# The three pieces of w_out converted inside the mixing steps, in the memory of theta's weights

## The chip, the cores and the metric

The kernel runs on one core of a Trainium2 chip. The metric is the device time of one execution in microseconds (us), the median of several runs; lower is better. The names of the engines are those of the profile: PE (matmul), PEld (its weight loads), DVE (vector), ACT (scalar), POOL (GpSimd) and SP, whose queue issues all the transfers.

## The reference, cut to what matters

Three layers follow each other. The first is an mLSTM-like attention with gates over 4 batches, 8 heads, 768 tokens and a head size of 40. Its output, 4 x 768 x 320, goes through a mixing layer, and that one's output through a gated convolution:

```python
theta = x @ w_theta                      # 320 x 320
zr, zi = x * cos(theta), x * sin(theta)
y = einsum('ts,bsd->btd', w_tok_r, zr) + einsum('ts,bsd->btd', w_tok_i, zi)   # 768 x 768 each
u = x + y
x = u + maximum(u @ w_ch, 0)             # 320 x 320
gate_pre = sum(conv_w[k] * x shifted by 4 - k tokens for k in range(5))
out = (sigmoid(gate_pre) * (x @ w_val)) @ w_out                               # 320 x 320 each
```

All weights arrive as 64-bit floating point numbers and are turned into 32-bit ones on the core. w_out is used by the last product alone.

## The kernel before, in words

The attention works through 12 groups (`attend(d)`; each is one batch's third of the tokens). Per group there are matrix products of gates (`weigh`), of keys and queries (`scores`), of states (`carry`, `inter`, `numer`), and a tail on DVE and POOL (`finish`). `weigh` ends in two exponentials on ACT, one for each half p of the heads (`W_m<-bank` or `x_b<-bank` in the profile).

The mixing layer has 24 steps (`step(n)`, recorded by two loops at the end): 2 pairs of batches (p), 2 halves of the output tokens, 6 chunks of the input tokens. A step issues 30 matmuls (`mix`, `bank<-wt_m,z` in the profile), and has the weights of the next step made (`weight`): for the first pair of batches a transfer of 64-bit numbers (`r_b<-in_wtok_dram`), ACT and DVE instructions that make 32-bit ones (`r_b<-r_b`) and split them into a high and a low part (`wt_m<-r_b`), and a transfer that keeps the parts in DRAM for the second pair (`wt_dr<-wt_m`). `theta(p, c)` makes the angles and with them z, the other operand of mix; for the first pair it reads w_theta from `w_t`. After six steps of a half its product with w_ch follows (`f_ch`), with DVE's convolution, then the one with w_val (`f_val`) and at last the one with w_out (`f_out`), each of them in the middle of the next half's mix steps.

The other weights are converted in 13 pieces by `cv_piece`: three of w_theta, the convolution's (cw), and three each of w_ch, w_val and w_out. A piece is a transfer of 320 KB (128 x 320 numbers of 8 bytes), one copy with scaling on ACT (`xq_m<-xq_m`), on DVE one TENSOR_SCALAR (shift) and two SCALAR_TENSOR_TENSOR (insert the low bits, insert the sign), and for w_ch, w_val and w_out another copy on ACT (`out_hi`) and a subtraction on DVE or POOL (`out_lo`). All pieces share two buffers in `xq_m`, used in turn.

The order of all this is not that of the code. Every call is recorded in a plan, and `Plan.order` lists the recorded steps: it takes costs, dependencies and due times (the time at which PE wants the result, worked back) and picks again and again the engine that is free first and its most urgent step. For some operations it also picks the engine (`any2`: DVE or POOL; `copy`: ACT or DVE). One table of the program acts on the pieces: `BY` says for a group of the attention which piece has to be done before the group's first exponential (`plan.follow`). Before, pieces 0 to 12 are all tied to groups 3 to 10, the last one to group 10. Each engine then carries out its own list in order.

Of the kernel before, what the change touches and what calls it, by code (L numbers as in the profile page):

```python
# [11 lines left out]
I64 = mybir.dt.int64  # L12
# [6 lines left out]
DM = H * D  # L19
# [10 lines left out]
WARM = 7  # L30
RFIRST = (1,)
GATES = (0, 2, 4)
BY = {3: 0, 4: 1, 5: 3, 6: 4, 7: 6, 8: 8, 9: 10, 10: 12}
U = L // 2
NU2 = S // U
FAR = -32768.0
# [311 lines left out]
def tile_kernel(ctx, tc, qT, kT, kt, v1, og, ig, fg, w_th, w_ch, w_val, w_out, cw, wtok,  # L348
# [12 lines left out]
    def turn(kind, n):  # L361

        turns[kind] = turns.get(kind, -1) + 1
        return turns[kind] % n

    def words(n, name, dtype=F32, place=None, bufs=1):

        t = sb.tile([128, n], dtype, name=name, tag=place or name, bufs=bufs)
        k = turn(place, bufs) if place else 0
        plan.place[t.name] = f"{place or name}.{k}"  # L370
        return t
# [12 lines left out]
    w_t = [words(n * DM, f"w_t{bb}").rearrange("p (k n) -> p k n", k=n) for bb, n in ((0, 3), (1, 1))]  # L384
# [34 lines left out]
    def cv_scale(raw, m):  # L419
        hi = raw.bitcast(I32).rearrange("p (n t) -> p n t", t=2)[:, :, 1]  # L420
        act.activation(out=m, in_=hi.bitcast(F32), func=AF.Copy, scale=REBIAS)

    def cv_bits(raw, m):
        w = raw.bitcast(I32).rearrange("p (n t) -> p n t", t=2)
        mi = m.bitcast(I32)
        dve.tensor_scalar(out=mi, in0=mi, scalar1=3, scalar2=None, op0=ALU.logical_shift_left)
        dve.scalar_tensor_tensor(out=mi, in0=w[:, :, 0], scalar=29, in1=mi,
                                 op0=ALU.logical_shift_right, op1=ALU.bitwise_or)
        dve.scalar_tensor_tensor(out=mi, in0=w[:, :, 1], scalar=-2147483648, in1=mi,
                                 op0=ALU.bitwise_and, op1=ALU.bitwise_or)  # L430
# [55 lines left out]
    def weigh(g):  # L486
# [8 lines left out]
        for p in range(2):  # L495
# [14 lines left out]
            act.activation(out=W[:, p], in_=G_ps, func=AF.Exp)  # L510
            if p == 0 and g in BY:
                plan.follow(made[BY[g]])
        st["W", g] = W
# [112 lines left out]
    def cv_piece(nm, src, k_):  # L626
        t = turn("cv", 2)
        raw = xq_m[:, (8 + 2 * t) * DM:(10 + 2 * t) * DM].bitcast(I64)
        v = xq_m[:, (12 + t) * DM:(13 + t) * DM]
        if nm == "cw":  # L630
            raw, v = raw[:, 0:15], cw_sb.rearrange("p j t -> p (j t)")
        sp.dma_start(out=raw, in_=src if nm == "cw" else src[:, k_ * DM:(k_ + 1) * DM])
        cv_scale(raw, v)
        cv_bits(raw, v)
        made.append(cw_sb[:] if nm == "cw" else w_t[0][0:64, k_] if nm == "th" else wsp[nm][1][:, k_])
        if nm == "cw":
            return
        if nm == "th":
            w0 = w_t[0][:, k_]
            if k_ == 2:  # L640
                pool.memset(w0[64:], 0.0)
                pool.memset(w_t[1][0:64], 0.0)
                act.activation(out=w_t[1][64:, 0], in_=v[64:], func=AF.Copy, scale=INV2PI)
                w0, v = w0[0:64], v[0:64]
            dve.tensor_scalar(out=w0, in0=v, scalar1=INV2PI, scalar2=None, op0=ALU.mult)
            return
        hi, lo = wsp[nm]
        act.activation(out=hi[:, k_, 0:DM], in_=v, func=AF.Copy)
        n = DM if nm == "out" else 256
        any2.tensor_tensor(out=lo[:, k_], in0=v[:, 0:n], in1=hi[:, k_, 0:n].bitcast(F32),  # L650
                           op=ALU.subtract)
        if n < DM:
            any2.tensor_tensor(out=hi[:, k_, DM:384], in0=v[:, 256:DM],
                               in1=hi[:, k_, 256:DM].bitcast(F32), op=ALU.subtract)

    pieces = [(nm, src, k_) for nm, src in (("th", w_th), ("ch", w_ch), ("val", w_val),
                                            ("out", w_out)) for k_ in range(3)]
# [256 lines left out]
    def mix(p, th_i, c, js=range(5)):  # L914
        z_hi, z_lo = st["z", p, c]
        w_hi, w_lo = st["w", p, th_i, c]
        for j in js:
            y = bank[j][:, 0:TH]
            with plan.joined():
                for ri in range(2):  # L920
                    zh, zl = blk(z_hi[:, ri], j), blk(z_lo[:, ri], j)
                    first = c == 0 and ri == 0
                    last = c == NC - 1 and ri == 1
                    pe.matmul(y, zh, w_hi[:, ri], start=first, stop=False)
                    pe.matmul(y, zh, w_lo[:, ri], start=False, stop=False)
                    pe.matmul(y, zl, w_hi[:, ri], start=False, stop=last)
# [53 lines left out]
    def f_u(p, th_i, bb):  # L980
        for j in ((0, 1, 4), (2, 3))[bb]:
            for g3 in (th_i, th_i + 1):
                a, e = max(0, 2 * g3 - 3 * th_i), min(3, 2 * g3 + 2 - 3 * th_i)
                i = 3 * th_i + a - 2 * g3
                old, y, new = (xq[p][:, 2 * g3:2 * g3 + 2, j, i * U:(i + e - a) * U].rearrange("p u (i l) -> p i u l", l=U),
                               *(t[:, a * L:e * L].rearrange("p (i u l) -> p i u l", u=2, l=U)
                                 for t in (bank[j], u_f[:, j])))
                dve.tensor_tensor(out=new, in0=old, in1=y, op=ALU.add)
        split(u_f, bb)
# [82 lines left out]
    def step(n):  # L1072

        half, k = divmod(n, NC)
        half -= 1
        fh = divmod(half, 2)
        if half == 2 and k == 0:
            both = words(12 * DM, "hl_x", F32R, place="x1")
            hl_x = both[:, 0:8 * TH].rearrange("p (s j t) -> p s j t", s=2, j=4)
            sr_x = both[:, 8 * TH:].rearrange("p (j t) -> p j t", j=2)  # L1080
            parts.append(part[:])
            part[:] = [[hl_x[:, s, 2 * bb:2 * bb + 2] for bb in range(2)] for s in range(2)] + [sr_x]
        if half >= 0 and k == 0:
            f_u(*fh, 0)
            f_u(*fh, 1)
        if 0 <= n < NS - 2:
            mix(*seq[n])
        elif n >= NS - 2:
            mix(*seq[n], (0, 1, 4))
        if half >= 0:  # L1090
            d = int(half == 0)
            if k == d:
                f_ch(*fh)
            elif k == 3 + d:
                f_val()
            elif k == 5 and half < 1:
                f_out(*fh, part, ob6)
        if 0 <= n + 1 < NS:
            weight(*seq[n + 1])
        if n == 7:  # L1100
            theta_weights()
        if n in first_use:
            theta(*first_use[n])

    parts = []
    todo = iter(pieces)
    for d in range(-1, NG):
        attend(d)
        for piece in [next(todo, None) for _ in range(1 + (d > 1 and d % 2 == 0))]:
# [3 lines left out]
    stage[0] = 1  # L1113
    for n in range(NS):
        step(n)
    stage[0] = 2

    parts.append(part[:])
# [82 lines left out]
```

## Time and profile before

| what | value |
|---|---|
| median of 3 runs | 398.55 us (396.32 to 399.29) |
| profiled execution | 394.67 us, of which its span is 392.8 us |
| PE busy | 355.9 us of the span |
| DVE, ACT, POOL busy | 328.8, 210.5, 95.1 us |
| TensorE clock granted, mean | 0.948 of 2.4 GHz |
| transferred | 57.74 MB |

The span is the time from the first instruction to the last on the profiled core. The profiled execution is 3.88 us under the median of the three timed runs.

The page's strip of 40 slices (9.8 us each) shows two stages: until about 147 us, where the attention goes on, PE is at 4 to 9 tenths; from about 150 us on it is full to the end, since the mix steps keep it so.

### The profile page before, as it was taken

The numbers are of one execution on the slowest core, as the hardware profiler recorded it, in microseconds if no ns is written. First come the engines' busy times: TensorE is split into PE (matmuls) and PEld (weight loads), VectorE is DVE, ScalarE is ACT, GpSimd is POOL, SyncE is SP. The second block draws the span as 40 slices with busy tenths as digits, with TensorE's granted clock in tenths as the row PEclk, the third lists the DMA queues.
The fourth block names the chain that finished last, engine by engine and source line by source line (L and its number), as shares of the span: only waits on it lengthen the run. The fifth ranks groups of instructions, "written<-read, shape, count | busy, mean of one in ns | idle before, by whom it ended". The sixth has DMA issues, their size and how long they took to land.

```text
span 392.8 us, 11329 instructions
## 1 busy us (share of the span) xinstructions
PE 355.9 (91%) x4736; PEld 325.0 (83%) x4736; DVE 328.8 (84%) x675; ACT 210.5 (54%) x373; POOL 95.1 (24%) x112
## 2 busy tenths in 40 slices
PE   4879888577878879999999999999999999999996
PEld 3556756466665658999999999999999999999996
DVE  7987959779989989999889988859987679468990
ACT  3655145025664776866544558865686332335463
POOL 8132322214646430100110033040022110213320
PEclk9585669988999999999999999999999999999999
DMA  5987749887655084969794184221320410000214
GB/s 168 301 230 216 210 139 244 204 227 202 195 164 147 9 237 119 294 192 270 210 300 164 61 257 163 85 81 38 124 82 18 152 73 0 2 0 2 101 38 164
DMA packets 22386, 57.74 MB, mean 147 GB/s; under 512 B 2912, under 2 KB 9216, under 8 KB 22336
## 3 DMA queue, kind: packets, MB, share of 16 engines
q1 hardware_dynamic: 22336, 57.03, 49.4%
q8 instruction: 37, 0.61, 0.7%
q14 instruction: 13, 0.11, 0.1%
HBM read 43.65 MB, written 13.37 MB: 145 GB/s over the span
## 4 chain that ended last, share of the span: by engine, by line
PE 52%; DVE 28%; ACT 8%; issue 7%; DMA 3%; POOL 0%; SPq 0%; ACTq 0%; DVEq 0%
PE bank L66 52%; DVE k_m L66 6%; DVE th_m L66 4%; DVE r_b L66 4%; DVE num_m L66 3%; DMA r_b<-in_wtok_dram 3%; ACT th_m L66 2%; DVE z L66 2%; DVE wt_m L66 1%; DVE xq_m L66 1%; ACT L66 1%; DVE g_m L66 1%; DVE f_m L66 1%; ACT W_m L66 1%; DVE W_m L66 1%
## 5 line engine op out<-in xcount | busy, mean ns | idle before, releaser
L66 PE MATMUL bank<-wt_m,z 128*128 128x384 f32 x480 | 87.6, 338 | 0.1
L66 PEld LDWEIGHTS bank<-wt_m,z 128*128 128x128 f32 x480 | 83.3, 188 | 0.8 <-DVE z L66 0.4
L66 PE MATMUL bank<-w_r,z 128*128 128x384 f32 x240 | 43.3, 336 | 0.0
L66 DVE SCALAR_TENSOR_TENSOR k_m<-k_m,cw_sb,k_m 128x384 f32<-128x384 f32 (+1 forms) x52 | 41.3, 830 | 0.4
L66 PEld LDWEIGHTS bank<-w_r,z 128*128 128x128 f32 x240 | 41.5, 188 | 0.0
L66 POOL TENSOR_TENSOR kw_m<-r_b,ewc 128x320 f32<-128x320 f32 x20 | 17.4, 873 | 40.6 <-PE bank L66 27.3
L66 PE MATMUL bank<-r_b,kw_m 64*64 64x41 f32 (+1 forms) x704 | 20.4, 236 | 7.1 <-DVE f_m L66 4.2
L66 PEld LDWEIGHTS bank<-r_b,kw_m 64*64 64x64 f32 (+1 forms) x704 | 17.4, 145 | 9.0 <-DVE f_m L66 4.3
L66 PE MATMUL bank<-q_m,k_m 64*64 64x64 f32 x768 | 18.8, 246 | 6.2 <-issue 5.8
L66 DVE SCALAR_TENSOR_TENSOR r_b<-r_b,r_b 128x768 int32<-128x768 int32 x24 | 23.7, 992 | 0.2
L66 DVE TENSOR_TENSOR k_m<-k_m,bank 104x164 f32<-104x164 f32 (+1 forms) x36 | 14.9, 420 | 9.4 <-PE bank L66 6.8
L66 PEld LDWEIGHTS bank<-q_m,k_m 64*64 64x64 f32 x768 | 16.5, 156 | 7.3 <-issue 6.2
L66 POOL TENSOR_TENSOR hl_f<-k_m,hl_f 128x768 fp32r<-128x768 f32 x4 | 8.1, 2030 | 55.8 <-ACT hl_f L66 55.8
L66 ACT ACTIVATE th_m<-bank,magic 128x320 f32<-128x320 f32 x24 | 12.5, 522 | 15.9 <-DVE th_m L66 9.0
L66 PE MATMUL bank<-w_t,xq_m 128*128 128x320 f32 x72 | 20.7, 437 | 0.3 <-ACT xq_m L66 0.3
L66 ACT ACTIVATE th_m<-th_m 128x640 f32<-128x640 f32 (+1 forms) x27 | 19.0, 702 | 3.3 <-DVE th_m L66 2.6
L66 ACT ACTIVATE z<-th_m 128x640 fp32r<-128x640 f32 x24 | 16.8, 730 | 6.2 <-DVE th_m L66 6.1
L66 ACT ACTIVATE W_m<-bank 128x512 f32<-128x512 f32 x16 | 9.3, 594 | 18.5 <-PE bank L66 18.5
L66 ACT ACTIVATE ewc<-bank 64x384 f32<-64x384 f32 x16 | 7.8, 486 | 21.1 <-PE bank L66 20.9
L66 ACT ACTIVATE xq_m<-bank 128x512 f32<-128x512 f32 (+2 forms) x36 | 14.7, 431 | 6.6 <-PE bank L66 5.5
L66 ACT ACT_TABLE_LOAD x14 | 18.0, 1283 | 0.3
L66 PEld LDWEIGHTS bank<-w_t,xq_m 128*128 128x128 f32 x72 | 13.4, 190 | 5.3 <-ACT xq_m L66 0.4
(207 smaller groups left out, 911.7 us busy)
## 6 DMA issues: line engine op xcount, KB each, us to landing
r_b<-in_wtok_dram SPq DMA_DIRECT2D x24, 384.0 KB
wt_dr<-wt_m SPq DMA_DIRECT2D x12, 768.0 KB
w_r<-wt_dr SPq DMA_DIRECT2D x8, 768.0 KB
r_b<-in_v_dram SPq DMA_DIRECT2D x12, 328.0 KB
q_m<-in_qT_dram SPq DMA_DIRECT2D x24, 160.0 KB
k_m<-in_kT_dram SPq DMA_DIRECT2D x24, 160.0 KB
r_b<-in_kt_dram SPq DMA_DIRECT2D x12, 320.0 KB
wt_m<-wt_dr SPq DMA_DIRECT2D x4, 768.0 KB
```

The source lines that it names most:

```text
L66: calls[u] = lambda e=e: getattr(e, op)(*args, **kw)
```

## The change

`cv_piece` gets other buffers for the three pieces of w_out: both the 64-bit numbers and the converted piece lie in `w_t[0]`, where theta's weights are for the first pair of batches. The three pieces have this one buffer among them, and none can be loaded before the last matmul that reads theta's weights there. Their recording moves from the attention's loop to mix steps 8, 9 and 10 (`OUT_AT`). The ten other pieces stay with the attention's groups, and `BY` spreads them over groups 3 to 10. The number of pieces and of their instructions stays as it is.

```diff
-BY = {3: 0, 4: 1, 5: 3, 6: 4, 7: 6, 8: 8, 9: 10, 10: 12}
+BY = {3: 0, 4: 1, 5: 2, 6: 4, 7: 5, 8: 7, 9: 8, 10: 9}
+OUT_AT = (8, 9, 10)
...
         t = turn("cv", 2)
         raw = xq_m[:, (8 + 2 * t) * DM:(10 + 2 * t) * DM].bitcast(I64)
         v = xq_m[:, (12 + t) * DM:(13 + t) * DM]
+        if nm == "out":
+            t3 = w_t[0].rearrange("p k n -> p (k n)")
+            raw, v = t3[:, 0:2 * DM].bitcast(I64), t3[:, 2 * DM:]
...
-    todo = iter(pieces)
+    todo = iter(pieces[:-3])
...
     for n in range(NS):
         step(n)
+        if n in OUT_AT:
+            cv_piece(*pieces[n - OUT_AT[0] - 3])
```

Since the plan is made anew, the order changes from the first microseconds on, on every engine; from the first w_ch product on, PE's order is the one of before. DVE's list has 671 instructions where it had 677, POOL's 120 for 117 and ACT's 383 for 375: some operations changed engines, and ACT's list has 20 loads of a function table where it had 15. Up to the end of the attention there are 15 of them for 10.

ACT around the exponentials of attention group 10 (`W_m<-bank_98` and `W_m<-bank_99`, its two halves; the `th_m<-th_m` rows are the sine and the absolute value of theta, `z` its result's high part). Before:

```order
L66 ACTIVATE th_m<-bank_98,magic 128x320
L66 ACTIVATE out_hi<-xq_m 128x320
L66 ACTIVATE z<-th_m 128x640
L66 ACTIVATE th_m<-bank_99,magic 128x320
L66 ACT_TABLE_LOAD
L66 ACTIVATE W_m<-bank_98 128x512
L66 ACTIVATE z<-th_m 128x640
L66 ACTIVATE W_m<-bank_99 128x512
L66 ACTIVATE r_b_81<-r_b_79 128x768
```

With the change:

```order
L67 ACTIVATE th_m<-bank_98,magic 128x320
L67 ACTIVATE th_m<-bank_99,magic 128x320
L67 ACTIVATE W_m<-bank_98 128x512
L67 ACT_TABLE_LOAD
L67 ACTIVATE th_m<-th_m 128x640 x2
L67 ACTIVATE th_m<-th_m,halfpi 128x640
L67 ACT_TABLE_LOAD
L67 ACTIVATE W_m<-bank_99 128x512
L67 ACTIVATE r_b_81<-r_b_79 128x768
```

Between the two halves of one group now stand two table loads and the three activations of a theta; `out_hi` is gone from here.

DVE just ahead of the last weights that it splits for the first pair of batches (`wt_m_107<-r_b_81`, made for mix step 11). Before:

```order
L66 TENSOR_TENSOR sr_f<-k_m_82,sr_f 64x384
L66 TENSOR_SCALAR r_b_81<-r_b_81 128x768
L66 SCALAR_TENSOR_TENSOR r_b_81<-r_b_80,r_b_81 128x768
L66 SCALAR_TENSOR_TENSOR th_m<-th_m,bank_105 128x256
L66 SCALAR_TENSOR_TENSOR th_m<-th_m,bank_105 128x64
L66 SCALAR_TENSOR_TENSOR r_b_81<-r_b_80,r_b_81 128x768
L66 TENSOR_TENSOR k_m_83<-k_m_83,bank_103 128x384
L66 TENSOR_TENSOR wt_m_107<-r_b_81,wt_m_107 128x768
```

With the change:

```order
L67 TENSOR_TENSOR sr_f<-k_m_82,sr_f 64x384
L67 TENSOR_SCALAR r_b_81<-r_b_81 128x768
L67 TENSOR_SCALAR w_t_70<-w_t_70 128x320
L67 SCALAR_TENSOR_TENSOR r_b_81<-r_b_80,r_b_81 128x768
L67 SCALAR_TENSOR_TENSOR w_t_70<-w_t_70 128x320
L67 SCALAR_TENSOR_TENSOR r_b_81<-r_b_80,r_b_81 128x768
L67 SCALAR_TENSOR_TENSOR th_m<-th_m,bank_105 128x256
L67 SCALAR_TENSOR_TENSOR th_m<-th_m,bank_105 128x64
L67 TENSOR_TENSOR k_m_83<-k_m_83,bank_103 128x384
L67 SCALAR_TENSOR_TENSOR w_t_70<-w_t_70 128x320
L67 TENSOR_TENSOR wt_m_107<-r_b_81,wt_m_107 128x768
```

The third piece's three instructions now stand among these; the first and the second stand in the same way earlier in the mix steps.

SP's queue in the mix steps with the change (`w_t_70<-in_w_out_dram` are the three pieces; `wt_m_106` and `wt_m_107` are the two buffers of the split weights). Before, the same transfers stand there without the pieces:

```order
L67 DMA r_b_79<-in_wtok_dram 64x2x384 x2
L67 DMA w_t_70<-in_w_out_dram 128x320
L67 DMA r_b_80<-in_wtok_dram 64x2x384 x2
L67 DMA wt_dr<-wt_m_106 128x1536
L67 DMA w_t_70<-in_w_out_dram 128x320
L67 DMA wt_dr<-wt_m_107 128x1536
L67 DMA r_b_79<-in_wtok_dram 64x2x384 x2
L67 DMA wt_dr<-wt_m_106 128x1536
L67 DMA r_b_80<-in_wtok_dram 64x2x384 x2
```

The second piece, which waits until the first is converted, now stands ahead of a store and of the next raw weights.

## Rows read from the trace of the kernel before

**Rows 1.** The page, part 1: busy time and share by engine.

```profile
PE 355.9 (91%) x4736; PEld 325.0 (83%) x4736; DVE 328.8 (84%) x675; ACT 210.5 (54%) x373; POOL 95.1 (24%) x112
```

**Rows 2.** Windows: stretch, length, busy us per engine, granted clock, DMA share, GB/s.

```profile
core 0: us, PE busy (x) PEld busy (x) DVE busy (x) ACT busy (x) POOL busy (x), PEclk, DMA share, GB/s
85.00:147.00 62.00, 51.21 (x1524) 39.42 (x1523) 58.56 (x137) 38.70 (x65) 29.89 (x35) 0.96 0.60 165
147.00:184.00 37.00, 36.95 (x197) 33.74 (x198) 35.96 (x63) 26.49 (x41) 1.68 (x2) 1.00 0.73 214
184.00:230.00 46.00, 46.00 (x270) 45.69 (x268) 42.56 (x68) 21.04 (x33) 4.45 (x4) 1.00 0.63 192
230.00:282.00 52.00, 50.97 (x320) 50.04 (x318) 43.16 (x82) 36.97 (x70) 11.02 (x10) 1.00 0.32 109
```

**Rows 3.** Groups of DVE's instructions, 85 to 184 us: busy, mean ns, idle before.

```profile
L66 DVE SCALAR_TENSOR_TENSOR xq_m<-xq_m 128x320 int32<-128x320 int32 x16 | 10.0, 626 | 0.1
...
L66 DVE TENSOR_SCALAR xq_m<-xq_m 128x320 int32<-128x320 int32 x8 | 4.2, 528 | 0.9 <-ACT xq_m L66 0.9
...
L66 DVE TENSOR_TENSOR out_lo<-xq_m,out_hi 128x320 fp32r<-128x320 f32 x1 | 0.5, 490 | 0.0
```

**Rows 4.** Timeline of DVE, single instructions of pieces: start, length.

```profile
108.46 0.32 DVE L66 TENSOR_SCALAR xq_m<-xq_m 128x320 int32<-128x320 int32 x1
...
120.48 1.81 DVE L66 TENSOR_SCALAR xq_m<-xq_m 128x320 int32<-128x320 int32 x1
...
122.62 0.48 DVE L66 SCALAR_TENSOR_TENSOR xq_m<-xq_m 128x320 int32<-128x320 int32 x1
```

**Rows 5.** Timeline of POOL beside them.

```profile
119.84 1.04 POOL L66 TENSOR_TENSOR k_m<-k_m,kw_m 104x164 f32<-104x164 f32 x1
...
120.84 1.26 POOL L66 TENSOR_TENSOR th_m<-th_m,x_a 128x512 f32<-128x512 f32 x1
```

**Rows 6.** Groups of DVE's instructions, 184 to 231 us.

```profile
L66 DVE TENSOR_TENSOR wt_m<-r_b,wt_m 128x768 fp32r<-128x768 f32 x6 | 5.7, 953 | 1.4 <-ACT wt_m L66 1.4
L66 DVE TENSOR_SCALAR r_b<-r_b 128x768 int32<-128x768 int32 x5 | 2.8, 559 | 1.1 <-ACT r_b L66 1.1
```

**Rows 7.** The page, part 5: table loads of ACT.

```profile
L66 ACT ACT_TABLE_LOAD x14 | 18.0, 1283 | 0.3
```

**Rows 8.** The chain that ended last: start, length; all its table loads.

```profile
55.86 1.28 ACT L66
...
59.90 1.28 ACT L66
...
126.72 0.97 ACT L66
...
236.03 1.28 ACT L66
```

**Rows 9.** Timeline of ACT around two loads.

```profile
104.45 0.53 ACT L66 ACTIVATE th_m<-bank,magic 128x320 f32<-128x320 f32 x1 [0.61 <-DVE th_m L66]
104.99 1.28 ACT L66 ACT_TABLE_LOAD   x1
106.28 0.60 ACT L66 ACTIVATE x_b<-bank 128x512 f32<-128x512 f32 x1
...
128.01 0.60 ACT L66 ACTIVATE W_m<-bank 128x512 f32<-128x512 f32 x1
...
129.13 0.59 ACT L66 ACTIVATE W_m<-bank 128x512 f32<-128x512 f32 x1
```

**Rows 10.** Timeline of PE: two of its waits after 147 us.

```profile
230.48 0.61 PE L66 MATMUL bank<-hl_f,val_hi 128*128 128x384 f32 x2 [0.20 <-DVE k_m L66]
...
281.80 0.44 PE L66 MATMUL bank<-id_sb,x 128*128 128x128 f32 x2 [0.70 <-DVE th_m L66]
```

**Rows 11.** Timeline of ACT: raw weights of mix steps that arrive late.

```profile
175.92 0.92 ACT L66 ACTIVATE r_b<-r_b 128x768 f32<-128x768 f32 x1 [1.94 <-DMA r_b<-in_wtok_dram]
...
183.05 0.90 ACT L66 ACTIVATE r_b<-r_b 128x768 f32<-128x768 f32 x1 [1.41 <-DMA r_b<-in_wtok_dram]
```

## The prediction

> **What bounds the kernel now.** I read the page first: PE is busy for 91% of the span and DVE for 84% [rows 1], so neither alone explains the end. The windows by stage come next, because the two shares are not spread evenly. From 147 to 230 us PE has no free time (36.95 of 37.00 and 46.00 of 46.00 us), while from 85 to 147 us it is busy for 51.21 of 62.00 us and DVE for 58.56 [rows 2]. The reader should see two limits here. In the last part of the attention DVE is 94% busy and PE leaves 10.79 us unused; after it PE is the limit, at a clock of 1.00, and whatever PE still has to do there keeps its length. So only two things move the end: how much idle time PE has until about 147 us, and whether PE has to wait again afterwards. The last view is PE's own waits after that point, two of which are 0.20 us at 230.48 and 0.70 us at 281.80, both for DVE [rows 10]. They are small, but they say that DVE is only just ahead of PE in the mix steps: it is busy for 35.96 of 37.00 us and for 42.56 of 46.00 us there [rows 2].
>
> **The change, term by term.**
>
> *What leaves DVE before 147 us.* Three pieces go: 3 TENSOR_SCALAR, 6 SCALAR_TENSOR_TENSOR, and one of the three subtractions (the other two were POOL's). At the means of 85 to 184 us, 0.528, 0.626 and 0.490 us [rows 3], that is 1.58 + 3.76 + 0.49 = 5.8 us. The same shift takes 0.32 us at 108.46 and 1.81 us at 120.48, where two of POOL's instructions run beside it, and the other form takes 0.48 us when nothing disturbs it [rows 4, 5]. At undisturbed lengths it is 0.96 + 2.88 + 0.49 = 4.3 us. I take 5.8, since the stage that they leave is the one with POOL busy for 29.89 us [rows 2], and since PE's idle 10.79 us there leave room for all of it. The bounds are 4.3 and 5.8.
>
> *What comes back on DVE between 147 and 230 us.* The same ten instructions, at undisturbed lengths because POOL is busy for just 1.68 and 4.45 us there [rows 2]: 4.3 us. The order puts the first piece before 184 us and the two others before the last `wt_m` split. DVE's free time in the two stretches is 1.04 + 3.44 = 4.48 us [rows 2]. If the pieces fit into it, they cost nothing; if each pushes what is behind it, 4.3 us. Of the 3.44 us, 1.4 and 1.1 us are waits for ACT's part of the weights [rows 6], which a piece ahead of them can fill, but the pieces' copies stand on ACT's list too. I take the middle, 2.2 us. What is late next, if they don't fit, is `wt_m` of steps 6 to 11, and behind it the mix matmuls.
>
> *Five more table loads on ACT*, 15 for 10 by the end of the attention. A load takes 1.283 us [rows 7]; nothing stands between it and its neighbours (104.98 us the end of the activation, 104.99 to 106.27 the load, 106.28 the next) [rows 9]. Five are 6.4 us. ACT is busy for 38.70 of 62.00 us in the stage where DVE binds [rows 2], so it has 23.3 us free, and the lower bound is nothing; the upper bound is all 6.4 us. The nearest row is the chain of waits: four loads stand on it, with 1.28 + 1.28 + 0.97 + 1.28 = 4.8 us of the 18.0 us that all 14 take, 27% [rows 7, 8]. At that share the five cost 1.7 us.
>
> The Trainium skill says otherwise on the price of a load (page "ScalarE: Activation LUTs", section "What ACT_TABLE_LOAD costs"): the load and a drain of 1380 ns make about 2.66 us for every switch. By that the five would be 13.3 us, an estimate, and 3.6 us at the same share, so that the sum would be 0 instead of -1.9. The trace agrees with its 1283 ns for the load, and shows no drain around it [rows 9].
>
> *The rest.* The six ACT copies of the pieces move from a stage with 23.3 us free to stretches where ACT is busy for 26.49 of 37.00 and 21.04 of 46.00 us: nothing, as long as ACT has that free time [rows 2]. Two subtractions stay on POOL, which is nearly empty there: nothing. Three transfers of 320 KB join SP's queue in the mix steps, 0.98 MB, or 4.6 us at the 214 GB/s of that stretch, with the DMA engines at 0.73 and 0.63 [rows 2]: nothing by the share, but the raw weights are already late there (1.94 and 1.41 us of waiting on ACT [rows 11]), so this is a rival below. The new ties of the ten other pieces only spread what the same groups waited for: nothing, covered by the time that groups wait for DVE anyway.
>
> *Sum:* -5.8 + 2.2 + 1.7 = -1.9 us. Against the profiled execution, 394.67 us, that is 392.8. That execution lies 3.88 us under the median of the runs, and I carry the same difference to the median: 398.55 - 1.9 = 396.7 us. With the bounds, -5.8 + 0 + 0 = -5.8 on one side and -4.3 + 4.3 + 6.4 = +6.4 on the other.
>
> **The rivals.**
>
> *A, all of it stays (faster).* The pieces find DVE's 4.48 free us in the mix steps and the loads find ACT's 23.3, so PE begins its full stretch 5.8 us earlier and is not held again: 398.55 - 5.8 = 392.8 us. For it speaks that the free time and the pieces are of one size [rows 2]; against it that DVE's free moments are waits for the weights' own path [rows 6], which the pieces lengthen.
>
> *B, the table loads take the place of DVE's work (slower).* The place is group 10. Before, its two exponentials start 1.12 us apart [rows 9]; now two loads and a theta's three activations stand between them. DVE multiplies both halves one after the other, and its whole list waits behind the second. If this load pair and the other three extra loads fall on the path in full, they cost 6.4 us, against 1.5 us that DVE saves when each piece pushes its neighbours (5.8 - 4.3): 398.55 + 4.9 = 403.4 us. It decides from the point where DVE has nothing ready to do while ACT loads: before, DVE is idle for 3.44 us of 62.00 there [rows 2], so any wait shows. Against it: just 27% of the loads stand on the chain now [rows 8], and the plan puts work ahead of such waits.
>
> *C, the change moves nothing.* The second w_out transfer waits in SP's queue until the first piece is converted, with a store and the raw weights of a later step behind it. Those weights already come 1.4 to 1.9 us late for ACT [rows 11]. If the queue is held for some 2 us and the delay goes through to PE, it eats the forecast's 1.9 us: 398.5 us.
>
> **How the numbers follow.** Forecast 0.47, with a range of its own of 394 to 399.5 us; A 0.22; B 0.17; C 0.14. The likeliest is 396.7 us. About 1% of 398.55 us, 4 us, is what a measurement can tell from no change here. Faster by over 1% (under 394.6) are A and the low end of the forecast: 0.22 + 0.06 = 0.28. Slower by over 1% (over 402.5) is B: 0.17. Within 1% is the rest: 0.41 + 0.14 = 0.55. The range goes from 392.0 to 402.5: it takes in A's time with 0.8 us to spare, and leaves out the farther part of A (0.07) and the larger part of B (0.12).
>
> **What would show it.** In the profile of the changed kernel: DVE's instructions on `w_t` by w_out between 165 and 230 us at about 0.32 and 0.48 us; PE's idle time between 85 and 147 us down from 10.79 by 3 to 5 us; 19 table loads in the page's group where 14 were, still 1.28 us each. The forecast is right in its terms if PE's first w_ch matmul comes 2 to 4 us earlier, and part of that is lost again by 230 us. It is wrong if DVE shows waits for ACT of more than a microsecond around group 10 (B), if ACT's waits for `r_b<-in_wtok_dram` grow by over 2 us in the mix steps (C), or if the first w_ch matmul and the end both come over 4 us earlier (A). A change in the first 85 us, where I have put nothing but two of the loads, would fall outside all of these.

## The result, and the profile after

The changed kernel takes 401.28 us (median of 5 runs, 399.19 to 403.41), the kernel before 398.52 us beside it (5 runs, 395.0 to 399.29): a measured ratio of 1.0134, 95% interval 1.0095 to 1.0173. It is slower: by 1.3% in this ratio, by 0.7% (2.8 us) if the two medians are compared. The profiled execution took 402.57 us, with a span of 400.6 us. A ratio in this document compares the undisturbed runs of both kernels, those at most 1.5% above the kernel's fastest, and the profiles of c0, e1, h_on, i1 and m1 below were taken on slower ones.

Page, part 1, and the group of table loads, the lines that answer to [rows 1, 7]:

```profile
PE 356.3 (89%) x4736; PEld 324.5 (81%) x4736; DVE 327.6 (82%) x669; ACT 218.9 (55%) x381; POOL 99.3 (25%) x115
...
L67 ACT ACT_TABLE_LOAD x19 | 24.4, 1283 | 0.3
```

The same four windows as [rows 2] (start and end, length, busy us of PE, PEld, DVE, ACT and POOL, granted clock, DMA share, GB/s):

```profile
85.00:147.00 62.00, 50.24 (x1542) 38.56 (x1543) 53.96 (x121) 35.78 (x54) 26.04 (x34) 0.89 0.45 122
147.00:184.00 37.00, 34.87 (x176) 29.73 (x176) 33.24 (x61) 28.00 (x44) 4.54 (x3) 1.00 0.75 208
184.00:230.00 46.00, 46.00 (x271) 45.96 (x270) 43.52 (x72) 21.32 (x34) 5.91 (x5) 1.00 0.74 232
230.00:282.00 52.00, 51.27 (x319) 50.61 (x318) 43.04 (x84) 37.70 (x70) 11.93 (x11) 1.00 0.35 112
```

The reader should see three things. DVE did lose work between 85 and 147 us (53.96 us where it had 58.56), but PE's idle time there did not shrink by the 3 to 5 us that the prediction wanted: it is 11.76 us, 62.00 less 50.24, where it was 10.79. The clock of that stretch fell from 0.96 to 0.89. And PE's full stretch begins later. In the mix steps the pieces are as cheap as forecast (DVE, single-instruction groups: duration least/median/most in ns, first and last start):

```profile
L67 DVE SCALAR_TENSOR_TENSOR w_t<-w_t x6: 481/484/493, 184.5 to 236.4; 128x320 int32<-128x320 int32 x6
L67 DVE TENSOR_SCALAR w_t<-w_t x3: 318/319/319, 184.1 to 233.1; 128x320 int32<-128x320 int32 x3
```

To see where the time went I cut both traces at the same events: DVE's first multiplication by the scores (`W_m<-W_m,bank` or `x_b<-x_b,bank`) of groups 0, 6 and 9 (counted from 0), PE's first mix matmul, and the end. Windows of before:

```profile
19.03:83.62 64.59, 49.74 (x1662) 39.38 (x1658) 50.44 (x133) 24.00 (x43) 18.07 (x26) 0.79 0.78 208
83.62:117.71 34.09, 28.25 (x956) 22.33 (x949) 32.22 (x84) 19.45 (x33) 16.21 (x22) 0.91 0.68 192
117.71:144.38 26.67, 22.84 (x609) 16.86 (x600) 25.10 (x52) 17.09 (x30) 12.87 (x14) 1.00 0.51 123
144.38:392.80 248.42, 242.90 (x1431) 237.56 (x1429) 205.44 (x359) 140.99 (x246) 38.73 (x35) 1.00 0.38 121
```

and of the changed kernel:

```profile
19.21:85.86 66.65, 46.00 (x1666) 36.38 (x1659) 49.08 (x132) 27.18 (x46) 21.34 (x28) 0.88 0.77 212
85.86:120.37 34.51, 27.41 (x885) 21.05 (x875) 29.94 (x72) 19.04 (x30) 16.83 (x25) 0.91 0.55 158
120.37:151.52 31.15, 25.69 (x659) 19.06 (x657) 25.92 (x53) 18.06 (x26) 9.21 (x9) 0.88 0.42 102
151.52:400.60 249.08, 243.58 (x1434) 238.18 (x1434) 206.76 (x367) 144.93 (x253) 42.73 (x37) 1.00 0.39 123
```

From the first mix matmul to the end the change costs 0.7 us. From group 9 to the first mix matmul, **the last stretch** below, it costs 4.5 us, and the clock there is 0.88 where it was 1.00. The cut at group 9 puts a little of PE's work on the other side (659 matmuls in the last stretch for 609); from group 6 to the first mix matmul, where this weighs less, 60.76 us became 65.66. The first window differs by 2.1 us, but no weight can be put on it: from group 0 to group 6 ten profiles with the new order there took 58.4 to 67.5 us (mean 63.6), seven with the old order 60.9 to 68.1 us (mean 64.6; m1 and m2, which add matmuls there, apart).

What happens in the changed kernel ahead of that clock is in PE's timeline (start, length, operation, count, and in brackets the idle time before it with its releaser):

```profile
117.43 0.96 PE L67 MATMUL bank<-r_b,kw_m 64*64 64x41 f32 x29 [2.79 <-DVE f_m L67]
...
133.54 0.66 PE L67 MATMUL bank<-r_b,kw_m 64*64 64x41 f32 x16 [2.43 <-DVE k_m L67]
```

and in DVE's, at the first of the two places:

```profile
113.75 1.89 DVE L67 TENSOR_TENSOR x<-x,num_m 128x640 f32<-128x640 f32 x1
115.57 0.84 DVE L67 TENSOR_TENSOR f_m<-f_m,kw_m 104x164 f32<-104x164 f32 x1
116.33 0.81 DVE L67 TENSOR_TENSOR x<-x,num_m 128x640 f32<-128x640 f32 x1
117.07 0.31 DVE L67 TENSOR_TENSOR f_m<-f_m,bank 104x164 f32<-104x164 f32 x1
120.37 0.69 DVE L67 TENSOR_TENSOR W_m<-W_m,bank 128x512 f32<-128x512 f32 x1 [1.12 <-PE bank L67]
```

The key products of the next group wait for a bank that DVE's `f_m<-f_m,bank` frees, and DVE first carries out two long multiplications (`x<-x,num_m`) of the group that is being finished. Behind the waiting products on PE's list stand the scores of group 9, so DVE's multiplication at 120.37 is late in turn. At 133.54 the same happens to group 10, whose second exponential is late too (the split that the prediction's rival B spoke of). ACT there:

```profile
128.14 0.60 ACT L67 ACTIVATE W_m<-bank 128x512 f32<-128x512 f32 x1 [0.41 <-PE bank L67]
128.76 1.28 ACT L67 ACT_TABLE_LOAD   x1
130.05 1.51 ACT L67 ACTIVATE th_m<-th_m 128x640 f32<-128x640 f32 x2
131.65 0.83 ACT L67 ACTIVATE th_m<-th_m,halfpi 128x640 f32<-128x640 f32 x1
132.50 1.28 ACT L67 ACT_TABLE_LOAD   x1
133.79 0.60 ACT L67 ACTIVATE W_m<-bank 128x512 f32<-128x512 f32 x1
```

And behind these waits PE's own work is slower. Windows of the changed kernel: the first wait and the work right behind it, the second wait and the work in two pieces behind it:

```profile
114.70:117.40 2.70, 0.00 (x0) 0.00 (x0) 2.70 (x5) 0.70 (x2) 1.01 (x2) 0.98 0.00 0
117.43:120.40 2.97, 2.97 (x96) 2.81 (x96) 1.78 (x5) 0.00 (x0) 2.11 (x3) 0.50 0.02 6
131.10:133.50 2.40, 0.00 (x1) 0.00 (x0) 2.37 (x4) 2.29 (x3) 2.40 (x2) 1.00 0.00 0
133.54:136.50 2.96, 2.77 (x80) 2.54 (x81) 1.41 (x4) 2.06 (x4) 2.12 (x4) 0.64 0.00 0
136.50:141.00 4.50, 3.73 (x50) 2.02 (x49) 4.47 (x6) 2.11 (x4) 1.54 (x1) 0.50 0.02 4
```

PE does nothing in the waits, and what follows falls to a granted clock of 0.50, the lower of its two levels (1.2 of 2.4 GHz). The same pair of matmuls in before, at a clock of 1.00, and in the changed kernel after the second wait:

```profile
132.53 0.38 PE L66 MATMUL bank<-k_m,b_m 128*128 128x256 bf16 x2
```

```profile
137.65 0.63 PE L67 MATMUL bank<-k_m,b_m 128*128 128x256 bf16 x2
```

### The profile page after: what moved, and what is told of

It is laid out like the page before. It is cut to its first block, busy times and chain, and to the rows that moved or that the text cites. A ratio compares the mean times of both kernels' runs of the same rounds, so it can differ in the third digit from the quotient of the medians.

```text
span 400.6 us, 11333 instructions
## 1 busy us (share of the span) xinstructions
PE 356.3 (89%) x4736; PEld 324.5 (81%) x4736; DVE 327.6 (82%) x669; ACT 218.9 (55%) x381; POOL 99.3 (25%) x115
## 4 chain that ended last, share of the span: by engine, by line
PE 55%; DVE 23%; issue 8%; ACT 7%; DMA 5%; POOL 1%; SPq 0%; ACTq 0%; DVEq 0%; POOLq 0%
PE bank L67 55%; DVE k_m L67 6%; DMA r_b<-in_wtok_dram 5%; DVE th_m L67 3%; DVE r_b L67 2%; DVE num_m L67 2%; ACT th_m L67 2%; ACT L67 2%; DVE x L67 1%; DVE xq_m L67 1%; DVE x_b L67 1%; DVE f_m L67 1%; DVE g_m L67 1%; DVE sr_f L67 1%; DVE W_m L67 1%
## 5 line engine op out<-in xcount | busy, mean ns | idle before, releaser
L67 PE MATMUL bank<-r_b,kw_m 64*64 64x41 f32 (+1 forms) x704 | 19.1, 232 | 11.0 <-issue 5.7
L67 PEld LDWEIGHTS bank<-r_b,kw_m 64*64 64x64 f32 (+1 forms) x704 | 16.5, 140 | 12.6 <-issue 6.2
L67 POOL TENSOR_TENSOR kw_m<-r_b,ewc 128x320 f32<-128x320 f32 x20 | 16.5, 823 | 40.7 <-PE bank L67 35.9
L67 PE MATMUL bank<-q_m,k_m 64*64 64x64 f32 x768 | 19.7, 252 | 7.4 <-issue 6.1
L67 ACT ACT_TABLE_LOAD x19 | 24.4, 1283 | 0.3
L67 PEld LDWEIGHTS <-k_m 128*64 128x64 bf16 (+1 forms) x224 | 10.7, 128 | 9.8 <-issue 8.3
L67 DVE TENSOR_TENSOR W_m<-W_m,bank 128x512 f32<-128x512 f32 x16 | 10.7, 682 | 9.7 <-PE bank L67 9.6
L67 POOL TENSOR_TENSOR th_m<-th_m,x 128x128 f32<-128x128 f32 (+1 forms) x8 | 7.4, 948 | 42.2 <-ACT th_m L67 42.2
```

Of the source, the lines that this page charges most:

```text
L67: calls[u] = lambda e=e: getattr(e, op)(*args, **kw)
```

## The experiments

In most of them the order is written out: a list of step numbers with their engines takes the place of the plan's result, so that one thing moves and nothing else.

```diff
+LIST = """s3 s4 v0 ..."""          # engine and number of every recorded step
+def issue(self):
+    for w in LIST.split():
+        for call in self.steps[int(w[1:])]["calls"][NAMES[w[0]]]:
+            call()
+Plan.issue = issue
```

The times of all runs, with the last stretch and its clock from each one's profile (old and new are the orders before and with the change). c0 is the changed kernel once more, with its order written out; c0, g1, h3 and i1 share one set of runs of before, so they are best compared with each other:

| run | attention's order | pieces in | last stretch, us | clock | first mix to end, us | ratio to before | 95% interval | medians of all runs, us: run / before beside it |
|---|---|---|---|---|---|---|---|---|
| before | old | attention | 26.67 | 1.00 | 248.4 | | | |
| changed | new | mix | 31.15 | 0.88 | 249.1 | 1.0134 | 1.0095 to 1.0173 | 401.28 / 398.52 |
| c0 | new | mix | 33.40 | 0.81 | 249.0 | 1.0198 | 1.0106 to 1.0290 | 402.92 / 396.38 |
| e1 | old | mix | 24.95 | 1.00 | 252.6 | 1.0033 | 0.9982 to 1.0085 | 400.68 / 396.92 |
| e2 | new | attention | 35.77 | 0.80 | 248.0 | 1.0321 | 1.0256 to 1.0385 | 409.99 / 396.92 |
| h_on | old, from group 6 new | mix | 33.29 | 0.81 | 249.1 | 1.0227 | 1.0146 to 1.0309 | 406.09 / 397.06 |
| h_no | new, from group 6 old | mix | 25.48 | 1.00 | 253.0 | 1.0088 | 1.0026 to 1.0149 | 399.59 / 397.06 |
| f5 | old | attention, no DVE work | 24.99 | 1.00 | 248.3 | 0.9939 | 0.9878 to 1.0000 | 397.09 / 397.06 |
| f6 | old | attention, DVE work twice | 32.81 | 0.84 | 248.4 | 1.0212 | 1.0128 to 1.0296 | 404.65 / 397.06 |
| i1 | planned with the old ties | mix | 23.21 | 0.90 | 253.9 | 1.0101 | 1.0034 to 1.0167 | 398.85 / 396.38 |
| e4 | new, exponentials together | mix | 29.60 | 0.88 | 248.9 | 1.0096 | 1.0053 to 1.0139 | 401.90 / 396.92 |
| e5 | new, 35 tiny matmuls ahead | mix | 32.39 | 0.80 | 250.2 | 1.0128 | 1.0070 to 1.0185 | 401.79 / 396.92 |
| g1 | new, state additions first | mix | 30.39 | 0.89 | 248.8 | 1.0235 | 1.0173 to 1.0297 | 401.53 / 396.38 |
| k2 | new, e4 and g1 together | mix | 31.12 | 0.84 | 247.8 | 1.0069 | 1.0026 to 1.0111 | 398.80 / 396.61 |
| k3 | new, k2 and scores first | mix | 32.02 | 0.83 | 248.0 | 1.0128 | 1.0069 to 1.0188 | 401.97 / 396.61 |
| k1 | new, matmuls in two waits | mix | 28.74 | 0.94 | 249.2 | 0.9894 | 0.9805 to 0.9983 | 398.28 / 396.61 |
| h3 | old to group 11, then new | mix | 28.27 | 0.94 | 248.4 | 1.0115 | 1.0051 to 1.0179 | 400.02 / 396.38 |
| h4 | old to third mix step, then new | mix | 24.70 | 1.00 | 249.7 | 0.9965 | 0.9924 to 1.0005 | 395.53 / 396.61 |
| m1 | h4, matmuls in two early waits | mix | 24.63 | 1.00 | 250.4 | 1.0003 | 0.9941 to 1.0065 | 395.61 / 397.84 |
| m2 | before, the same matmuls | attention | 28.25 | 0.94 | 248.9 | 1.0018 | 0.9949 to 1.0086 | 397.26 / 397.84 |

**Order or move.** e1 takes the changed code and the order of before for all steps but the pieces', e2 the reverse.

> The changed code, its pieces of w_out in the mix steps, but every other step on every engine in the order of the kernel before (15 table loads, the two exponentials of group 10 side by side). Theory 1, the loss comes from the order that the plan made anew: this runs no slower than the kernel before (398.5 us), 394 to 398 us, since DVE is rid of 4.3 to 5.8 us in the attention and gets back nearly nothing that costs in the mix steps. Theory 2, moving the pieces costs by itself (their transfers, their copies, the wait for the memory of theta's weights): 400.5 to 403 us, about the changed kernel's 401.3.

> The mirror image: the code of before, its pieces in the attention, but every other step in the order of the changed kernel (20 table loads, group 10's exponentials split). Theory 1, the order: no faster than the changed kernel, 401 us if the pieces fit into the 6.2 us in which DVE is idle from 85 to 110 us, up to 406 us if they push what is behind them. Theory 2, the moving: back to about 398.5 us.

In the last stretch the loss goes with the order: 24.95 us in e1, 35.77 in e2. e2 is the slowest kernel of all, though its pieces never moved; part of that is likely the pieces' work, put back into an order in which no place was made for it. But e1 did not gain, as theory 1 wanted: 1.0033, and 400.68 us for 396.92 by the medians, nowhere near 394 us. What it saves in the last stretch it loses after the first mix matmul, 252.6 us for 248.4. PE's waits of e1 in the mix steps (who waits for whom, us in total, times, longest):

```profile
PE bank L67 <- DVE z L67: 1.2, 1, 1.2
PE bank L67 <- DVE k_m L67: 1.1, 2, 0.6
PE bank L67 <- DVE xs_lo L67: 0.6, 1, 0.6
PE bank L67 <- ACT z L67: 0.6, 1, 0.6
```

So where the order of the mix steps was not made for the pieces, they push what PE needs by 4 us; in the changed kernel's own order they cost 0.7 us.

**What the removed work was worth.** f5 leaves the nine instructions out (w_out stays unconverted), f6 issues each twice; in the list:

```diff
-... v495 v496 v497 ... v561 v562 v563 ... v604 v605 v606 ...
+(f5: these nine left out; f6: each of them twice)
```

> The kernel before in its own order; the nine instructions on DVE that convert w_out's three pieces (three shifts, six that insert bits) are left out, so w_out stays unconverted; the pieces' transfers, ACT's copies and the subtractions stay where they are. This takes away the work that the prediction counted as a gain, and nothing comes back later. If DVE is the limit of the attention's last part, as the prediction had it, 3.8 to 5.3 us faster than before. If what limits it is the chain between PE and DVE, group after group, with DVE's work on pieces only filling the time in which it waits for PE: 0 to 2 us faster.

> The kernel before in its own order; each of the same nine instructions on DVE is issued twice in a row (w_out's conversion then gives other numbers). If DVE is the limit there: 3.8 to 5.3 us slower than before. If its time on the pieces is time in which it would wait for PE anyway: less than 2.5 us slower, though more than leaving them out gains, since the waits that a piece can fill are then full.

Leaving them out gives 0.6%, 2.4 us (0 to 4.9), and the median of all runs of f5, 397.09 us, is that of before beside it, 397.06 us. Windows of f5 from group 6 to 9 and from there to the first mix matmul:

```profile
82.06:116.68 34.62, 28.84 (x950) 22.45 (x940) 30.49 (x81) 18.80 (x32) 13.66 (x21) 0.90 0.67 192
116.68:141.67 24.99, 22.74 (x610) 16.87 (x600) 22.51 (x47) 17.60 (x30) 13.36 (x15) 1.00 0.52 130
```

DVE works for 53.00 us there where it worked for 57.32, and the two stretches take 59.61 us where they took 60.76: of the 4.3 us of work that are gone, 3.2 us have become idle time of DVE. f6 fits neither of its expectations: the doubling costs 2.1%, 8.4 us (7.6 by the medians), for some 5 us of work, and the clock of the last stretch goes from 1.00 to 0.84 with it. So the work fills time in which DVE would mostly wait, but more of it is not free.

**Which half of the order.**

> The changed kernel with its pieces in the mix steps; up to group 6's multiplication with the weights (about 84 us) every step stands as in the kernel before, from there on as in the changed kernel. Where the loss of the new order (about 1.3% to before, and 0.3% with the old order throughout) comes from: all of it before that cut gives 0.3%, about 1.2 us over before; all of it after the cut gives 1.3%, about 5 us over before; an even split lies between, 2.5 to 3.5 us over before.

> The mirror image: up to the same step the order of the changed kernel, from there on that of the kernel before, the pieces in the mix steps. Loss before the cut: about 5 us over before; loss after the cut: about 1.2 us over before.

The loss lies after the cut: 1.0227 with the new order there, 1.0088 with the old one, whose last stretch is 25.48 us (its 253.0 us from the first mix matmul on are near e1's).

**Fetches.** e5 shifts PE's list:

```diff
     for n in range(WARM):
-        pe.matmul(bank[6 + n % 2][:, 0:256], ...)
+        with plan.joined():
+            pe.matmul(bank[6 + n % 2][:, 0:256], ...)
+            for _ in range(5):
+                pe.matmul(bank[6 + n % 2][0:32, 0:8], num_m[:, 0:32], num_m[:, 0:8], ...)
```

> The changed kernel in its own order; each of its seven warm-up matmuls at the start is followed by five tiny ones (32 x 8), so that PE's list is 140 instructions longer ahead of the attention and nothing else moves. They cost about 3 us of PE before 10 us, where 3.5 us are idle. If the idle time that the profile puts down to issue (16.8 us from 13 to 147 us, in pieces of up to 4.4 us in the middle of a group of like matmuls) depends on where in the list PE runs out of instructions, the places move by half the distance between two of them and the time changes by over 1 us to either side, with other groups cut. If those gaps belong to the order and its waits, they stay in the same groups and the time is within 0.7 us of 401.3.

The gaps did move: in the changed kernel one of 4.36 us stood at 66.69 us, in e5 the largest is at 70.18, in another group, and from 13 to 147 us they sum to 11.9 us, not 16.8.

```profile
66.69 0.49 PE L67 MATMUL bank<-r_b,kw_m 64*40 64x41 f32 x10 [4.36 <-issue]
```

```profile
70.18 0.25 PE L67 MATMUL bank<-f_m,q_m 64*64 64x41 f32 x2 [2.78 <-issue]
```

The time did not move (1.0128), but this alone proves little: e5's added matmuls also start group 0 late, at 22.48 us for 19.21. What speaks against the gaps as the loss is c0, the same instructions as the changed kernel: its gaps sum to 12.2 us, about those of before (12.3), and it is no faster. In the last stretch the changed kernel and c0 have none, and before has 1.0 us.

**One wait at a time.** e4 and g1 each undo one wait of the last stretch (order of the changed kernel with - and +):

```diff
 ACT W_m<-bank (group 10, first half)
+ACT W_m<-bank (second half)                 e4
 ACT th_m<-th_m x2, th_m<-th_m,halfpi
-ACT W_m<-bank (second half)
...
+DVE f_m<-f_m,kw_m, f_m<-f_m,bank            g1, group 8; k_m<-k_m,bank in the same way at group 10
 DVE x<-x,num_m, x<-x,num_m
-DVE f_m<-f_m,kw_m, f_m<-f_m,bank
```

> The changed kernel in its own order, but for one step on ACT: group 10's second exponential stands next to the first, ahead of theta's three activations; the number of table loads stays. Rival (table loads and the split pair of group 10 make the loss): the 2.8 us by which this group fell further behind (from 2.7 us at group 9 to 5.5 us) come back, 398.3 to 399.5 us. Theory 1 with the loss spread over stalls and waits of PE before it: within 0.7 us of the changed kernel's 401.3.

> The changed kernel in its own order, but for DVE at two places: the additions to the running state that free the banks of the next group's key products (f_m<-f_m,kw_m and f_m<-f_m,bank at group 8, k_m<-k_m,bank at group 10) stand ahead of the two multiplications x<-x,num_m of the group that is being finished, and not behind or between them. Nothing else moves; 20 table loads stay. In the changed kernel PE waits 2.79 and 2.43 us for these additions, and behind its waiting products stand the scores of the next group. Theory, these places make the loss: DVE is idle for 1.12 and 1.44 us ahead of the next groups' W_m<-W_m,bank, so 2.5 us come back, and a little more if PE's clock stays high in between: 397.5 to 399.5 us where the changed kernel has 401.3 (ratio to before 1.000 to 1.007). If the loss is elsewhere (table loads, fetches): within 0.7 us of the changed kernel, ratio 1.012 or more.

> The changed kernel with its order written out, instruction for instruction the same on every engine. It says how the changed kernel stands to the kernel before on the chip on which the other three run: ratio 1.010 to 1.017.

e4's stretch is 29.60 us, g1's 30.39, against 31.15 and 33.40 in the two profiles of the changed kernel: each a little shorter, neither at 27, and shorter than the first of the two by less than these differ. In time e4 is within the changed kernel's interval and level with e5 by the medians (401.90 and 401.79 us). g1, 1.0235, is not faster than c0 beside it, 1.0198, so the theory that these two places alone make the loss failed. c0 itself came out above the 1.010 to 1.017 expected.

**Both waits, and the clock by itself.** k2 makes both moves; k3 in addition puts the scores of groups 9 and 10 ahead of the waiting products on PE. k1 moves nothing and gives PE something to do in the waits:

```diff
+    plan.fill = lambda: tc.nc.tensor.matmul(bank[0][:, 0:L], id_sb, id_sb, start=True, stop=True)
...
     for w in LIST.split():
+        for _ in range(7 if w in ("p627", "p669") else 0):
+            self.fill()
```

> The changed kernel in its own order, with seven matmuls (128x128, their result is overwritten by the next scores) put on PE's list at two places, ahead of the key products that wait for DVE's f_m<-f_m,bank at group 8 (2.79 us) and k_m<-k_m,bank at group 10 (2.4 us). Nothing waits less. If the clock that falls behind these waits is the larger part of the loss: a granted clock of 0.93 or more from group 9's W multiplication to the first mix matmul (0.81 to 0.88 in the changed kernel), that stretch 28 to 30 us where it has 31.2 and 33.4 us, and a ratio of 1.003 to 1.010. If the waits are the loss and the clock only follows from other things: stretch 31 to 34 us, ratio 1.012 or more.

> The changed kernel in its own order with both earlier moves at once: group 10's exponentials side by side on ACT, and the state additions ahead of the multiplications x<-x,num_m on DVE at groups 8 and 10. If the two waits at group 10 stand side by side (the scores wait for the second exponential by their bank and stand behind the key products that wait for DVE): the stretch from group 9's W multiplication to the first mix matmul falls to 26.5 to 28.5 us (29.6 and 30.4 us with one move alone), its clock is 0.93 or more, ratio 1.000 to 1.007. If not: 29 to 30 us, clock below 0.9, ratio as with one move alone, 1.010 or more.

> As the run with both moves, and in addition the scores of groups 9 and 10 stand ahead of the waiting key products on PE, and group 10's W multiplication ahead of x<-x,num_m on DVE: the order in which the kernel before has these steps. If these places hold all of the loss: the stretch 25 to 27 us as with the order of before, clock 0.95 or more, ratio 0.995 to 1.003. If something else in the new order holds it: 28 us or more.

k1's clock and stretch came out as the clock's theory said: 0.94 and 28.74 us. Windows of the last stretch, of k1 and of c0:

```profile
113.77:142.51 28.74, 25.80 (x673) 19.55 (x671) 23.78 (x54) 17.98 (x26) 11.57 (x10) 0.94 0.43 99
```

```profile
122.68:156.08 33.40, 28.14 (x659) 21.33 (x657) 26.16 (x53) 18.07 (x26) 9.36 (x10) 0.81 0.39 96
```

k1's PE needs 25.80 us, 1.83 us of it for the added matmuls, for the work on which c0 spends 28.14. Its ratio, 0.9894, rests on two of six runs; the median of all six is 398.28 us, of before beside it 396.61. So k1 is not shown to beat before; it does lie under the changed kernel in either reading, though by the medians just by 0.3% (1.0042 for 1.0069). The clock is not all kept: behind the second place PE still waits for DVE (0.65 and 0.85 us), and from 128.6 to 132.5 us the clock is 0.61. k2's time is half of the loss lower (1.0069), but its stretch is not shorter (31.12 us): there PE waits in new places, for the multiplication itself and in a gap of issue.

```profile
132.03 0.58 PE L67 MATMUL bank<-k_m 128*128 128x512 bf16 x1 [2.33 <-DVE W_m L67]
...
143.57 0.43 PE L67 MATMUL bank<-r_b,x_b 64*64 64x41 f32 x12 [2.11 <-issue]
```

k3 traded the waits for a larger one, of group 11's scores for ACT:

```profile
142.51 1.73 PE L67 MATMUL bank<-q_m,k_m 64*64 64x64 f32 x38 [6.40 <-ACT x_b L67]
```

So k3 does not bear out my claim that these places hold all of the loss; with its new wait it is no clean test of it either.

**What the move can be worth.**

> The pieces of w_out in the mix steps; the order of the kernel before up to the last group's W multiplication (about 138 us), the order of the changed kernel from there on, where its plan has found room for the pieces. With the old order throughout, the pieces cost about 4 us of PE's waiting in the mix steps (3.7 us between 172 and 240 us), in the changed kernel 0.2 us. If what the attention gains by losing the pieces is the 2.4 us measured without their work on DVE, and the mix steps cost nearly nothing: 395 to 396.5 us, ratio to before 0.992 to 0.998, and faster than both kernels. If the mix steps cost as much as with the old order: ratio 1.003 to 1.008.

> Pieces in the mix steps; the order of before until the third mix step's first half (about 175 us), the order of the changed kernel from there on. From group 9 to the first mix matmul 25 us as with the old order, from the first mix matmul to the end 245.6 to 246.4 us as in the changed kernel. By the intervals measured so far that is 1 to 2 us under the kernel before: ratio 0.995 to 1.000, about the most that the move can give. If moving the pieces costs the old order something outside these stretches: 1.003 to 1.010.

> The move of the pieces alone: the table that ties pieces to the attention's groups is that of before for the ten that stay (groups 3 to 8 as they were, the last of w_val with group 10); the plan makes its own order. It has 15 table loads again. On DVE one of the two multiplications x<-x,num_m still stands ahead of each of the two state additions at group 8, and one ahead of that at group 10. If the new spread of the ties made the loss: ratio 0.997 to 1.003. If moving the pieces makes the plan find such an order whatever the ties: ratio 1.008 to 1.015.

h3 was cut at a bad place: between the two orders PE waits 3.80 us for ACT ahead of theta's matmuls, and the gain is gone.

```profile
140.29 1.77 PE L67 MATMUL bank<-w_t,xq_m 128*128 128x320 f32 x4 [3.80 <-ACT xq_m L67]
```

h4, cut later, has the ratio and the last stretch that were expected: 0.9965 (395.53 us, 12 runs, before 396.61 beside it) and 24.70 us. From the first mix matmul on it takes 249.7 us, near the changed kernel's 249.1; the 245.6 to 246.4 us in the expectation were a wrong figure for that kernel. With the mix steps ordered as in the changed kernel from the third on, the old order ahead of them takes the loss away, so h4 is the plainest sign that the order makes it. It beats the changed kernel; against before its interval reaches 1.0005. i1 moves the pieces and leaves the old ties to the rest (`BY = {3: 0, 4: 1, 5: 3, 6: 4, 7: 6, 8: 8, 10: 9}`). It fits neither expectation: without the new ties the last stretch is the shortest of all, 23.21 us, but 5.4 us are lost after it, and the ratio is 1.0101. So this plan loses in a place of its own.

**The clock where it is lowest.** m1 and m2 put six matmuls before each of two waits of groups 1 and 2, in the same way as k1.

> The kernel with the pieces in the mix steps, the order of before until the third mix step and that of the changed kernel from there on (ratio 0.9965), with six matmuls (128x128, their result is overwritten) put on PE's list at each of two places where PE waits for DVE: ahead of group 1's second key products (1.8 us, f_m) and ahead of group 2's products with x_b (1.9 us, num_m). If PE's clock behind waits is what the time hangs on there too: granted clock from group 0's to group 6's W multiplication 0.83 or more (0.79), that stretch 61 to 63 us (64.9), ratio 0.986 to 0.994. If not, 0.995 to 0.999.

> The kernel before in its own order, pieces in the attention, with the same twelve matmuls at the same two places. If the clock is what the time hangs on there: that stretch 61 to 63 us where it has 64.6, ratio 0.990 to 0.997. If not, 0.998 to 1.002. Against the other run it lies 0.3% higher if the move is worth what it was without the matmuls.

A miss. The clock from group 0 to group 6 rose from 0.79 to 0.91 and 0.92, and the times stayed within their intervals (1.0003 for h4's 0.9965, and 1.0018 for before). m1's first stretch stayed (65.01 us for h4's 64.91); m2's fell from 64.59 to 61.11, within what profiles of the old order differ by, and m2 loses it again up to the first mix matmul (66.77 us from group 6 on, before 60.76). Windows of m1, groups 0 to 6 and 6 to 9:

```profile
18.88:83.89 65.01, 47.55 (x1696) 38.28 (x1691) 52.01 (x134) 24.01 (x43) 18.23 (x26) 0.91 0.74 206
83.89:122.63 38.74, 30.06 (x949) 23.91 (x940) 29.60 (x81) 18.23 (x31) 12.34 (x20) 0.87 0.57 157
```

PE is idle for 17 us of the first of them; its speed does not seem to be what the groups wait for there. By these runs a higher clock is worth something only where the others wait for PE.

## Why the prediction was wrong

Predicted were 396.7 us, 1.9 us faster; measured are 401.28 us, 2.8 us slower by the medians and 1.3% in the ratio. Two steps failed: the first term was mis-sized, and the new order, put at nothing beyond its table loads, costs 4.5 us in the last stretch.

- *What leaves DVE, -5.8 us.* With the order held it is worth some 2.4 us (0 to 4.9, f5, which leaves out nine of the ten instructions), not 5.8; the lower bound, 4.3, is not excluded by the times. I had read DVE's 58.56 of 62.00 us as a limit [rows 2]. It was a full engine, not the one that all waited for: part of its work could only fill waits that come back when the work goes. In f5 3.2 of 4.3 us did. In the changed kernel DVE waits 6.8 us for PE's scores ahead of the multiplications `W_m<-W_m,bank` of groups 6, 7, 9 and 10, where it waited 2.6 us. "PE's idle 10.79 us there leave room for all of it" counted the room and did not ask what each piece of it waits for.
- *The order, which had no term.* I costed the new plan by its table loads, and the new ties at "nothing, covered by the time that groups wait for DVE anyway"; with the old ties (i1) the last stretch takes 23.21 us, with the new ones 31.15 and 33.40. What it also moved, state additions behind long multiplications on DVE and scores behind waiting products on PE, stood in its list and was not followed. That is where the sign turned: the last stretch takes 24.6 to 26.7 us with the old order (before, e1, f5, h_no, h4, m1; 28.3 in m2, whose clock was 0.94), 28.7 to 33.4 us with the new one and the pieces in the mix steps. Against the old order with the pieces moved (24.6 to 25.5 us) the changed kernel's 31.15 and 33.40 us are 5.7 to 8.8 us more.
- *The clock.* The sum had none, since it is 1.00 from 147 us on. In the last stretch it is 1.00 in six of seven profiles with the old order there (f6, with its doubled work, and h3, which changes over inside it, apart), and 0.80 to 0.94 in all nine with the new one and the pieces moved. The Trainium skill (page "TensorE: Matmul & The Clock Gate", section "HAM oscillation — how this bites in real kernels") describes the like for longer waits, for transfers: each makes the next group of matmuls start at the lower clock. The trace agrees in kind: a clock of 0.50 behind waits of 2.79 and 2.43 us, and 0.63 us for 0.38.
- *What comes back, 2.2 us, bounds 0 and 4.3.* The durations were right (0.319 and 0.484 us), the bounds too: from the first mix matmul to the end 0.7 us more in the changed kernel, 4.2 in e1. Which of them holds was the plan's doing.
- *Table loads, 1.7 us.* 19 loads at 1283 ns, as forecast; what they cost by themselves no run shows. Rival B had one of the right places. But ahead of group 10's multiplication DVE waits for PE's scores (1.44 us), not for ACT, and e4, without the split, gains nothing clear of the noise (1.0096 for 1.0134, with overlapping intervals). So its reason, two loads between two exponentials, is at best a part of the loss.
- *Rival C* did not happen: from the first mix matmul to 285 us ACT waits 3.1 us for raw weights, where it waited 4.4 us, and the whole costs 0.7 us.

What stays open is how the loss splits between waits and clock. The profiles show both parts: from group 6 to the first mix matmul PE is busy for 53.10 us with 1544 matmuls (55.94 in c0) where it was for 51.09 us with 1565, and idle for 12.56 us (13.31) where it was for 9.67. k1 suggests that the clock is a good part, k2 and k3 that mending single waits brings up others.

## What to carry to other kernels

An engine that is 94% busy need not be the limit: ask what waits for it at each point, and price work that leaves it by what becomes free behind it. Less work and more work need not cost alike: here leaving it out gave some 2.4 us, and doubling it cost 8.4. Where a planner re-orders everything after a small edit, the new order is the change: hold the order to measure the edit, and hold the edit to measure the order. In the new list look on each engine for short steps that free a buffer and now stand behind long ones, and for what is queued behind their waiter.

## What the runs showed of the hardware

- The changed kernel and c0 are the same instructions; in the last stretch PE was busy for 25.69 us at a clock of 0.88 in one profile and 28.14 us at 0.81 in the other, and the stretch took 31.15 and 33.40 us. A single profile of such a kernel is not its time.
- PE stands still for up to 4.36 us in the middle of a group of like matmuls, waiting for nothing but issue. The page counts 37 transfers on the queue of instructions (0.61 MB, 16 KB each), and the gap of 4.36 us ends 1.4 us after one of them has landed. Five of c0's six gaps over 0.5 us stand at the same matmuls, though with other lengths; e5's, with 140 instructions more ahead of them, stand at others. So the likely cause is that PE runs out of instructions. The Trainium skill (page "Runtime: NRT & Kernel Launch", section "Instruction fetch mechanics") calls the crossing of such a block mostly hidden; if that is the cause, it was not hidden here, among matmuls of 64x41 and 64x64.
